# FFN forward with F tiles outermost, the activations through DRAM, and the output product in a stage of its own

## The chip, the cores and the metric

The kernel runs on one core of a Trainium2 chip. The metric is the device time of one execution in microseconds (us). TensorE (PE) multiplies, VectorE (DVE) and ScalarE (ACT) work on tiles in SBUF and PSUM, GpSimd (POOL) and SyncE (SP) issue DMA transfers here. A DMA is queued by the engine that issues it, so there are queues of SP, ACT and POOL.

## The reference

Forward and backward of one block, for L = 2048 tokens, D = 576 channels, F = 4608 hidden units and N = 128 states; inputs and outputs are bf16.

```
xn  = layernorm(u)
s   = S4 state space model: long convolution of xn with a kernel made of A, B, C, log_dt, plus Dskip * xn
ffn(x) = (silu(x @ w1) * (x @ w3)) @ w2          # w1, w3: D x F, w2: F x D
g   = silu(ffn(xn))
out = u + s * g
outputs: out and the gradients of all inputs for a given grad_out
```

## The kernel before

The phases follow each other in this order: constants, layernorm, parameters and the convolution kernel, the convolution itself by DFT blocks (phase 3; its last matmuls are L607, inv_ps), the FFN forward (phase 4, which the change rewrites), the backward pass of the state space model (phase 5), the backward pass of the FFN (phase 6: weight gradients, then input gradients). xn lies transposed in DRAM as XNT_dram. D = 576 is four blocks of 128 and a rest of 64, F is 36 tiles of 128.

Phase 4 before (L637 to L764) goes over four chunks of 512 tokens, and in each over the 36 F tiles (fi). For one F tile and each half of 256 tokens, five matmuls with w1res (L697) and five with w3c (L700) accumulate the two products in one PSUM tile gu; the last of the five uses a block whose lower 64 rows are zero. ScalarE makes the sigmoid and two bf16 copies (L704 to L706), VectorE two products (L708, L709) that give hT. Both copies go to G_dram and U_dram for phase 6. For each of the four token tiles of the chunk hT is then multiplied with this F tile's rows of w2 (w2r): 512 columns into o_main (L714) and 64 into o_tail (L718). w1 is resident (w1res), loaded at the start by 72 DMAs; w3c and w2r are loaded again in each chunk, with a memset by GpSimd for w3c's zero rows. At the end of a chunk there is an epilogue for four token tiles (L722 to L755): copies, a sigmoid (L732), eight passes on VectorE per tile that give out, gs_t and go_o (the gradients that phases 5 and 6 need, stored to GS_dram and GO_dram), and transposes of go_o (L761) that are stored to GOT_dram.

Phase 5 starts with the DFT matrices Cf, Sf and others: VectorE and ScalarE compute them by rows (L416 to L440), and PE transforms gs with them (dft_ps, L496). Phase 6 reads G_dram and U_dram (L1177, L1189), makes ph (L1209), the weight gradients pgw (L1238, L1250, and L1257 and L1259 for the last 64 rows) and the input gradient px (L1302).

`self.dma` (L77) gives its transfers to SP's and ACT's queue by turns. The order of instructions on each engine is made by a scheduler from the program's order; tiles come from pools, and a pool that is opened later can lie on the addresses of one that is closed.

Of the kernel before, what the change touches and what calls it, by code (L numbers as in the profile page):

```python
# [60 lines left out]
class K:  # L61
# [561 lines left out]
    def load_wcols(self, pool, w_ap, f0, fw, name, eng=None):  # L623
        nc, cfg = self.nc, self.cfg
        D, DT = cfg.D, cfg.DT
        t_ = pool.tile([P, DT, fw], BF16, name=name)
        nfull = D // P
        rem = D - nfull * P
        if rem > 0:
            nc.gpsimd.memset(t_[rem:P, DT - 1, :], 0.0)  # L630
        if nfull > 0:
            self.dma(t_[:, 0:nfull, :], w_ap[0:nfull * P, f0:f0 + fw].rearrange("(c p) f -> p c f", p=P), eng=eng)
        if rem > 0:
            self.dma(t_[0:rem, nfull, :], w_ap[nfull * P:D, f0:f0 + fw], eng=eng)
        return t_

    def phase4_ffn_fwd(self):  # L637
# [3 lines left out]
        TCW = min(512, L)  # L641
        NTC = L // TCW
        TS = TCW // P
        HW = TCW // 2
        assert TCW % 2 == 0 and HW <= 256
        opieces = [(0, min(512, D))] + ([(512, D - 512)] if D > 512 else [])
        assert D <= 1024
        self.G_dram = self.dram.tile([FT, P, L], BF16, name="G_dram")
        self.U_dram = self.dram.tile([FT, P, L], BF16, name="U_dram")
        self.GS_dram = self.dram.tile([P, LT, D], BF16, name="GS_dram")  # L650
        self.GO_dram = self.dram.tile([P, LT, D], BF16, name="GO_dram")
        self.GOT_dram = self.dram.tile([P, DT, L], BF16, name="GOT_dram")
# [3 lines left out]
        with self.tc.tile_pool(name="f_big", bufs=1) as big, \  # L656
                self.tc.tile_pool(name="f_w", bufs=3) as wpool, \
                self.tc.tile_pool(name="f_gu", bufs=3) as gup, \
                self.tc.tile_pool(name="f_h", bufs=2) as hpool, \
                self.tc.tile_pool(name="f_ep", bufs=2) as ep, \  # L660
                self.tc.tile_pool(name="f_ep1", bufs=2) as ep1, \
                self.tc.tile_pool(name="f_goo", bufs=TS) as goop, \
                self.tc.tile_pool(name="f_pso", bufs=TS, space=bass.MemoryType.PSUM) as pso, \
                self.tc.tile_pool(name="f_pst", bufs=1, space=bass.MemoryType.PSUM) as pst, \
                self.tc.tile_pool(name="f_psg", bufs=2, space=bass.MemoryType.PSUM) as psg, \
                self.tc.tile_pool(name="f_pstr", bufs=1, space=bass.MemoryType.PSUM) as pstr:
            xnT = big.tile([P, DT, L], BF16, name="xnT4")
            for c in range(DT):
                self.dma(xnT[:, c, :], self.XNT_dram[:, c, :])
            w1 = big.tile([P, DT, F], BF16, name="w1res")  # L670
            nfull = D // P
            rem = D - nfull * P
            if rem > 0:
                nc.vector.memset(w1[rem:P, DT - 1, :], 0.0)
            for ft in range(FT):
                if nfull > 0:
                    self.dma(w1[:, 0:nfull, ft * P:(ft + 1) * P],
                             aps["B_w1"][0:nfull * P, ft * P:(ft + 1) * P].rearrange("(c p) f -> p c f", p=P))
                if rem > 0:
                    self.dma(w1[0:rem, nfull, ft * P:(ft + 1) * P], aps["B_w1"][nfull * P:D, ft * P:(ft + 1) * P])  # L680
            for tci in range(NTC):
                t0 = tci * TCW
                o_main = [pso.tile([P, 512], FP32, name="o_main") for _ in range(TS)]
                o_tail = pst.tile([P, TS, 64], FP32, name="o_tail") if len(opieces) > 1 else None
                for fi in range(FT):
                    f0 = fi * P
                    w3c = self.load_wcols(wpool, aps["B_w3"], f0, P, "w3c")
                    w2r = wpool.tile([P, D], BF16, name="w2r")
                    self.dma(w2r[:], aps["B_w2"][f0:f0 + P, :])
                    hT = hpool.tile([P, TCW], BF16, name="hT")  # L690
                    gsp = gup.tile([P, TCW], BF16, name="g_sp")
                    usp = gup.tile([P, TCW], BF16, name="u_sp")
                    for hh in range(2):
                        tsl = slice(t0 + hh * HW, t0 + (hh + 1) * HW)
                        gu = psg.tile([P, 2, HW], FP32, name="gu")
                        for c in range(DT):
                            nc.tensor.matmul(gu[:, 0, :], lhsT=w1[:, c, f0:f0 + P], rhs=xnT[:, c, tsl],  # L697
                                             start=(c == 0), stop=(c == DT - 1))
                        for c in range(DT):
                            nc.tensor.matmul(gu[:, 1, :], lhsT=w3c[:, c, :], rhs=xnT[:, c, tsl],  # L700
                                             start=(c == 0), stop=(c == DT - 1))
                        hs = slice(hh * HW, (hh + 1) * HW)
                        sig = gup.tile([P, HW], BF16, name="sig")
                        nc.scalar.activation(out=sig[:], in_=gu[:, 0, :], func=ACT.Sigmoid)  # L704
                        nc.scalar.copy(out=gsp[:, hs], in_=gu[:, 0, :])  # L705
                        nc.scalar.copy(out=usp[:, hs], in_=gu[:, 1, :])  # L706
                        silu = gup.tile([P, HW], BF16, name="silu")
                        nc.vector.tensor_tensor(out=silu[:], in0=gsp[:, hs], in1=sig[:], op=ALU.mult)  # L708
                        nc.vector.tensor_tensor(out=hT[:, hs], in0=silu[:], in1=usp[:, hs], op=ALU.mult)  # L709
                    self.dma(self.G_dram[fi, :, t0:t0 + TCW], gsp[:])  # L710
                    self.dma(self.U_dram[fi, :, t0:t0 + TCW], usp[:])
                    for ts in range(TS):
                        (po, pw) = opieces[0]
                        nc.tensor.matmul(o_main[ts][:, 0:pw], lhsT=hT[:, ts * P:(ts + 1) * P], rhs=w2r[:, po:po + pw],  # L714
                                         start=(fi == 0), stop=(fi == FT - 1))
                        if o_tail is not None:
                            (po, pw) = opieces[1]
                            nc.tensor.matmul(o_tail[:, ts, 0:pw], lhsT=hT[:, ts * P:(ts + 1) * P], rhs=w2r[:, po:po + pw],  # L718
                                             start=(fi == 0 and ts == 0), stop=(fi == FT - 1 and ts == TS - 1))
# [697 lines left out]
```

## Time and profile before

| | before |
|---|---|
| median of three runs | 3525.78 us (3524.29 to 3532.9) |
| profiled execution | 3535.09 us, its span 3533.3 us |
| PE busy | 2430.8 us, 69% of the span |
| VectorE busy | 1961.1 us, 56% |
| ScalarE busy | 1601.8 us, 45% |
| GpSimd busy | 221.5 us, 6% |
| mean granted clock of PE | 0.774 |
| DMA | 368.13 MB, 104 GB/s in the mean |

The profile and the trace are of one execution. Busy time is the time in which an engine has an instruction; a granted clock of 1.00 is 2.4 GHz, 0.5 is 1.2 GHz. Phase 4 lies between about 802 and 1445 us of the span.

### The profile page before, as it was taken

What the parts mean: (1) busy time and instruction counts of PE and PEld (TensorE: products, weight loads), DVE (VectorE), ACT (ScalarE), POOL (GpSimd) and SP (SyncE); (2) the same over time, 40 slices, a digit from 0 to 9 for tenths busy, and PEclk for the clock granted to TensorE, in tenths of its full rate; (3) what the DMA queues carried; (4) which work ended last, traced back from release to release, by engine and by line L of the source; (5) the groups of instructions that cost most, each with busy time, mean ns of one, the idle gap of its engine ahead of it and who ended that gap; (6) DMA issues with size and microseconds to landing.
All of it is one profiled execution on the core that took longest, in us unless ns stands there. A gap on an engine that the chain in (4) does not pass through costs nothing.

```text
span 3533.3 us, 53058 instructions
## 1 busy us (share of the span) xinstructions
PE 2430.8 (69%) x20638; PEld 1645.3 (47%) x20638; DVE 1961.1 (56%) x3182; ACT 1601.8 (45%) x2617; POOL 221.5 (6%) x518
## 2 busy tenths in 40 slices
PE   2999994836988979373632111117999998973999
PEld 1444442624655656162421111105677776752777
DVE  6777777582344343847579999983444433410222
ACT  2888885402544545441106655626565665510000
POOL 1000000000000000000000000001222222210000
PEclk8555555968988999596765555558999999986999
DMA  2000000206566565301124333317544544437442
GB/s 75 20 21 21 22 22 20 108 19 180 152 177 171 157 173 155 115 1 53 42 52 114 99 100 100 98 26 212 152 139 133 145 143 132 117 95 190 166 176 78
DMA packets 431854, 368.13 MB, mean 104 GB/s; under 512 B 210929, under 2 KB 395762, under 8 KB 429426
## 3 DMA queue, kind: packets, MB, share of 16 engines
q10 hardware_dynamic: 204000, 182.79, 16.9%
q1 hardware_dynamic: 208018, 122.94, 13.5%
q0 software_dynamic: 19584, 59.00, 5.3%
q8 instruction: 162, 2.65, 0.3%
q14 instruction: 90, 0.74, 0.1%
HBM read 214.81 MB, written 133.27 MB: 99 GB/s over the span
## 4 chain that ended last, share of the span: by engine, by line
PE 50%; DVE 26%; issue 9%; DMA 7%; SPq 3%; POOL 2%; ACT 2%; ACTq 0%; POOLq 0%; DVEq 0%
PE px L1302 8%; PE o_main L714 4%; PE ph L1209 4%; PE gu L700 4%; PE gu L697 4%; PE tau_ps L353 4%; PE e_ps L356 3%; PE dft_ps L496 3%; SPq L1114 3%; DVE prodI L1006 2%; PE gk_ps L866 2%; DVE red L1014 2%; PE e_ps L365 2%; DMA out_dram<-gw 2%; PE pgw L1238 2%
## 5 line engine op out<-in xcount | busy, mean ns | idle before, releaser
L993 PE MATMUL pT<-gK,QTr 64*128 64x32 bf16 x576 | 72.6, 185 | 295.8 <-DVE QTr L979 269.5
L708 DVE TENSOR_TENSOR silu<-g_sp,sig 128x256 bf16<-128x256 bf16 x288 | 83.8, 292 | 344.1 <-ACT g_sp L705 343.7
L1302 PE MATMUL px<-w1T,ggc 128*128 128x288 bf16 x1152 | 238.1, 289 | 49.5 <-DMA w3T<-in_B_w_dram 41.8
L697 PE MATMUL gu<-xnT,w1res 128*128 128x256 bf16 x1440 | 229.8, 275 | 46.3 <-ACT u_sp L706 33.6
L1302 PE MATMUL px<-w3T,guc 128*128 128x288 bf16 x1152 | 237.8, 289 | 32.3 <-DMA guc<-GU_dram 20.2
L1250 PEld LDWEIGHTS <-xn_bf 128*128 128x128 bf16 x2304 | 226.0, 99 | 58.1 <-issue 30.3
L704 ACT ACTIVATE sig<-gu 128x256 bf16<-128x256 f32 x288 | 110.5, 384 | 272.9 <-PE gu L700 234.7
L700 PE MATMUL gu<-xnT,w3c 128*128 128x256 bf16 x1440 | 228.8, 275 | 0.0
L993 PEld LDWEIGHTS <-QTr 64*128 64x128 bf16 x1152 | 65.0, 101 | 319.1 <-DVE QTr L979 273.7
L1209 PE MATMUL ph<-go_oT,w2T 128*128 128x512 bf16 x720 | 169.5, 381 | 60.8 <-DMA w2T<-w2r 58.2
L714 PE MATMUL o_main<-w2r,hT 128*128 128x512 bf16 x576 | 188.3, 395 | 9.6 <-DVE hT L709 2.4
L1253 DVE CAST gw<-pgw 128x256 bf16<-128x256 f32 x144 | 60.1, 423 | 229.5 <-DMA out_dram<-gw 125.9
L1306 DVE TENSOR_TENSOR gx<-px,gx 128x288 f32<-128x288 f32 x32 | 13.1, 452 | 306.6 <-PE px L1302 200.6
L1319 ACT ACTIVATE t<-gx 128x576 f32<-128x576 f32 x16 | 10.9, 683 | 374.5 <-DVE gx L1306 374.5
L1238 PE MATMUL pgw<-go_o,h_n 128*128 128x288 bf16 x1152 | 165.1, 286 | 0.0
L697 PEld LDWEIGHTS <-w1res 128*128 128x128 bf16 x1440 | 131.6, 98 | 71.1 <-issue 35.6
L1250 PE MATMUL pgw<-gg_n,xn_bf 128*128 128x256 bf16 x1152 | 133.4, 276 | 27.1 <-DVE gw L1253 27.1
L1302 PEld LDWEIGHTS <-ggc 128*128 128x128 bf16 x1152 | 113.6, 99 | 80.1 <-issue 50.6
L700 PEld LDWEIGHTS <-w3c 128*128 128x128 bf16 x1440 | 132.9, 99 | 30.6
L353 PE MATMUL tau_ps<-SELQ,thp 64*128 64x512 f32 x144 | 143.2, 1096 | 0.3 <-ACT WiT L242 0.3
L1302 PEld LDWEIGHTS <-guc 128*128 128x128 bf16 x1152 | 113.5, 99 | 63.4 <-DMA guc<-GU_dram 20.8
L356 PE MATMUL e_ps<-SELQ,rho 64*128 64x512 f32 x144 | 137.5, 1057 | 0.0
(358 smaller groups left out, 6667.8 us busy)
## 6 DMA issues: line engine op xcount, KB each, us to landing
rep_t<-RT_dram SPq DMA_DIRECT2D x72, 256.0 KB, 4.1
rep_r<-RT_dram ACTq DMA_DIRECT2D x72, 256.0 KB, 3.9
gate<-G_dram POOLq DMA_DIRECT2D x36, 512.0 KB, 4.7
up<-U_dram POOLq DMA_DIRECT2D x36, 512.0 KB, 6.2
GU_dram<-guT ACTq DMA_DIRECT2D x36, 512.0 KB, 3.3
GG_dram<-ggT ACTq DMA_DIRECT2D x36, 512.0 KB, 6.5
ggc<-GG_dram ACTq DMA_DIRECT2D x8, 2304.0 KB, 8.8
guc<-GU_dram ACTq DMA_DIRECT2D x8, 2304.0 KB, 14.2
```

The source lines that it names most:

```text
L353: nc.tensor.matmul(pt[:], lhsT=self.thp[rows, c, :], rhs=SELQ[rows, cols], start=True, stop=True)
L356: nc.tensor.matmul(pe[:], lhsT=self.rho[rows, c, :], rhs=SELQ[rows, cols], start=True, stop=True)
L496: nc.tensor.matmul(pt[:, 0:pw], lhsT=mat[:, tt, kc * P:(kc + 1) * P], rhs=src_fn(tt)[:, po:po + pw], start=(tt == 0), stop=(tt == KT - 1))
L697: nc.tensor.matmul(gu[:, 0, :], lhsT=w1[:, c, f0:f0 + P], rhs=xnT[:, c, tsl], start=(c == 0), stop=(c == DT - 1))
L700: nc.tensor.matmul(gu[:, 1, :], lhsT=w3c[:, c, :], rhs=xnT[:, c, tsl], start=(c == 0), stop=(c == DT - 1))
L704: nc.scalar.activation(out=sig[:], in_=gu[:, 0, :], func=ACT.Sigmoid)
L714: nc.tensor.matmul(o_main[ts][:, 0:pw], lhsT=hT[:, ts * P:(ts + 1) * P], rhs=w2r[:, po:po + pw], start=(fi == 0), stop=(fi == FT - 1))
L993: nc.tensor.matmul(pT[:, gi, kind, :], lhsT=lhs[rows, dl, :], rhs=rhs[rows, dp, :], start=True, stop=True)
L1209: nc.tensor.matmul(ph[:, q * 512:(q + 1) * 512], lhsT=w2T[:, c, :], rhs=go_oT[:, c, hh * HL + q * 512:hh * HL + (q + 1) * 512], start=(c = ...
L1238: nc.tensor.matmul(pgw[pi_][:, 0:pw], lhsT=h_ns[fl][:, tt, :], rhs=go_o[:, tt, po:po + pw], start=(tt == 0), stop=(tt == LT - 1))
L1250: nc.tensor.matmul(pw_[:, 0:GW], lhsT=self.xn_bf[:, tt, c * P:(c + 1) * P], rhs=nat[:, tt, :], start=(tt == 0), stop=(tt == LT - 1))
L1302: nc.tensor.matmul(px[pi_][:, 0:pw], lhsT=act[:, fi, k * P:(k + 1) * P], rhs=wT[:, fi, po:po + pw], start=(fi == 0 and ai == 0), stop=(fi ...
```

## The change

Phase 4 is split in two. The first part (phase4_hidden) takes one F tile after the other, and for each all 2048 tokens in two halves of 1024: the two products are made in PSUM tiles pg and pu (two banks each, two buffers each), with matmuls of 512 columns (L683). The rest of 64 rows of D is no longer padded with zeros: w1's 64 rows lie on partitions 0 to 63 and w3's on 64 to 127 of one tile (wtail), xnT's last 64 rows are loaded to both halves of the partitions, and the K=64 matmuls for pg (L686) and pu (L688) use the two row halves of the array. ScalarE makes Silu directly (L690) and copies pu (L692), VectorE copies pg (L691) and makes the product (L693) for 2048 tokens. The product is stored to H_dram (L694, SP's queue, runs of 512 bytes), g_t and u_t to G_dram and U_dram (POOL's queue, 512 KB each). The weights of four F tiles come in one group of loads on SP; w2 is loaded into w2res (41 KB per partition) by nine loads on POOL's queue.

The second part (phase4_output) loads H_dram again, 256 tokens of all F tiles at a time (hc, eight loads of 2304 KB, three buffers), and for each of 16 token tiles does 72 matmuls of 288 columns with w2res (L727). The epilogue follows for each tile, with five transposes a tile (L752). The buffers of phase 5's DFT matrices lie on addresses of w2res; before, they lay on addresses of w1res and xnT4.

```diff
-            for tci in range(NTC):
...
                 for fi in range(FT):
-                    w3c = self.load_wcols(wpool, aps["B_w3"], f0, P, "w3c")
-                    self.dma(w2r[:], aps["B_w2"][f0:f0 + P, :])
...
-                    for hh in range(2):
-                        for c in range(DT):
-                            nc.tensor.matmul(gu[:, 0, :], lhsT=w1[:, c, f0:f0 + P], rhs=xnT[:, c, tsl],
-                                             start=(c == 0), stop=(c == DT - 1))
...
-                    for ts in range(TS):
-                        nc.tensor.matmul(o_main[ts][:, 0:pw], lhsT=hT[:, ts * P:(ts + 1) * P], rhs=w2r[:, po:po + pw],
-                                         start=(fi == 0), stop=(fi == FT - 1))
...
+            for fi in range(FT):
+                if fl == 0:
+                    for w in ("B_w1", "B_w3"):
+                        nc.sync.dma_start(out=wm[w][:], in_=aps[w][0:nfull * P, f0:f0 + GRP * P].rearrange(
...
+                    nc.gpsimd.dma_start(out=self.w2res[:, fi:fi + GRP, :],
...
+                for hh in range(L // HL):
+                    for (w, pt) in (("B_w1", pg), ("B_w3", pu)):
+                        for c in range(nfull):
+                            for (o, t0) in qs:
+                                nc.tensor.matmul(pt[:, o:o + 512], lhsT=wm[w][:, c, cs], rhs=xnT[:, c, t0:t0 + 512],
+                    for (o, t0) in qs:
+                        nc.tensor.matmul(pg[:, o:o + 512], lhsT=wt[0:rem, cs], rhs=xnT[0:rem, nfull, t0:t0 + 512],
+                        nc.tensor.matmul(pu[:, o:o + 512], lhsT=wt[rem:P, cs], rhs=xnT[rem:P, nfull, t0:t0 + 512],
+                    nc.scalar.activation(out=s_t[:, hs], in_=pg[:], func=ACT.Silu)
+                    nc.vector.tensor_copy(out=g_t[:, hs], in_=pg[:])
+                    nc.scalar.copy(out=u_t[:, hs], in_=pu[:])
+                nc.vector.tensor_tensor(out=h_t[:], in0=s_t[:], in1=u_t[:], op=ALU.mult)
+                nc.sync.dma_start(out=self.H_dram[:, :, fi, :].rearrange("c p l -> p c l"),
+                nc.gpsimd.dma_start(out=self.G_dram[fi], in_=g_t[:])
+                nc.gpsimd.dma_start(out=self.U_dram[fi], in_=u_t[:])
...
+            for i in range(LT):
+                if k == 0:
+                    nc.sync.dma_start(out=hc[:], in_=self.H_dram[i // (TC // P)])
...
+                for fi in range(FT):
+                    for pi_, (po, pw) in enumerate(pieces):
+                        nc.tensor.matmul(po_[:, pi_, 0:pw], lhsT=hc[:, fi, k * P:(k + 1) * P],
+                                         rhs=self.w2res[:, fi, po:po + pw], start=(fi == 0), stop=(fi == FT - 1))
```

On PE, inside a chunk, the kernel before has these rows (numbers of tiles behind a name are those of the program):

```order
L700 LDWEIGHTS w3c
L700 MATMUL gu<-xnT_6805,w3c 128x256
L697 LDWEIGHTS w1res
L697 MATMUL gu<-xnT_6805,w1res 128x256
L697 LDWEIGHTS w1res
L697 MATMUL gu<-xnT_6805,w1res 128x256
L714 LDWEIGHTS hT
L714 MATMUL o_main<-w2r,hT 128x512
L718 LDWEIGHTS hT
L718 MATMUL o_tail<-w2r,hT 128x64
L714 LDWEIGHTS hT
L714 MATMUL o_main<-w2r,hT 128x512
L718 LDWEIGHTS hT
L718 MATMUL o_tail<-w2r,hT 128x64
L697 LDWEIGHTS w1res
L697 MATMUL gu<-xnT_6805,w1res 128x256
```

The products of the next half stand between those of hT with w2r, and half of the matmuls with hT have 64 columns. In the changed kernel PE has these rows at the end of one half and the start of the next:

```order
L683 LDWEIGHTS wmB_w_6798
L683 MATMUL pu<-xnT_6789,wmB_w_6798 128x512
L686 LDWEIGHTS wtail
L686 MATMUL pg<-xnT_6789,wtail 128x512
L688 LDWEIGHTS wtail
L688 MATMUL pu<-xnT_6789,wtail 128x512
L686 LDWEIGHTS wtail
L686 MATMUL pg<-xnT_6789,wtail 128x512
L688 LDWEIGHTS wtail
L688 MATMUL pu<-xnT_6789,wtail 128x512
L683 LDWEIGHTS wmB_w_6796
L683 MATMUL pg<-xnT_6789,wmB_w_6796 128x512
```

All matmuls have 512 columns; the K=64 ones stand in turns, pg and pu, between those of two halves, and no product with w2 is left here.

On VectorE, at the end of phase 4, the kernel before has the last tile of a four-tile epilogue (24 rows of the other three tiles stand ahead of it) and then rows of the DFT matrices:

```order
L742 TENSOR_TENSOR t1e<-s_t_15374,g 128x576
L747 TENSOR_TENSOR gs_t<-go_t,g 128x576
L744 TENSOR_TENSOR o_15380<-t1e,x_t 128x576
L750 SCALAR_TENSOR_TENSOR e<-o_sb,g 128x576
L753 TENSOR_TENSOR t1e<-go_t,s_t_15374 128x576
L752 TENSOR_TENSOR e<-e,sgo 128x576
L425 TENSOR_SCALAR g_u<-g_u 128x512
L755 TENSOR_TENSOR go_o<-t1e,e 128x576
L427 SCALAR_TENSOR_TENSOR g_fr<-g_tau,g_u 128x512
L416 TENSOR_SCALAR g_prod<-irow,tcolv 128x512
```

The DFT rows L425, L427 and L416 stand behind the four tiles. In the changed kernel the same place reads:

```order
L467 TENSOR_SCALAR tcolv<-pcol 128x1
L458 TENSOR_SCALAR w_10761<-w_10761 128x1
L810 TENSOR_TENSOR gsxn<-gs,xn_bf 128x576
L735 TENSOR_TENSOR g<-po,sgo 128x576
L416 TENSOR_SCALAR g_prod<-irow,tcolv 128x512
L736 SCALAR_TENSOR_TENSOR e<-po,g 128x576
L744 TENSOR_TENSOR gs_t<-go_t,g 128x576
L739 TENSOR_TENSOR e<-e,sgo 128x576
L746 TENSOR_TENSOR g<-s_t_10628,g 128x576
L741 TENSOR_TENSOR go_o<-gos,e 128x576
L748 TENSOR_TENSOR o_10721<-g,x_t 128x576
L419 TENSOR_SCALAR g_q<-g_prod 128x512
```

Only one tile's epilogue stands here; a product with gs (gsxn) and the first DFT rows stand ahead of it and in it.

On GpSimd the changed kernel has these rows where the kernel before has only memsets of w3c, 144 of them:

```order
L668 DMA w2res<-in_B_w_dram 128x4x576 x8
L697 DMA U_dram<-u_t 128x2048
L696 DMA G_dram<-g_t 128x2048
L668 DMA w2res<-in_B_w_dram 128x4x576
L721 DMA x_t<-in_A_u_dram 128x576
L722 DMA go_t<-in_grad_out_dram 128x576
L723 DMA s_t_8979<-S_dram 128x576
L721 DMA x_t<-in_A_u_dram 128x576
L722 DMA go_t<-in_grad_out_dram 128x576
```

Eight of nine loads of w2res stand ahead of the first store of an F tile, and loads of the epilogue's inputs for the first tiles stand behind it.

## Rows read from the trace of the kernel before

**Rows 1.** Windows, start of the stage; us, then busy us (count) per engine, clock, DMA.

```profile
804.50:845.00 40.50, 11.37 (x59) 7.14 (x59) 3.35 (x9) 4.88 (x13) 0.40 (x2) 0.58 0.81 211
845.00:960.00 115.00, 111.94 (x889) 73.01 (x890) 36.85 (x127) 58.66 (x192) 6.37 (x32) 1.00 0.61 164
960.00:1000.00 40.00, 23.77 (x172) 15.55 (x172) 27.67 (x56) 17.34 (x49) 0.99 (x5) 0.74 0.66 190
```

**Rows 2.** Timeline of PE, start of the stage; start us, us, instruction, [idle before].

```profile
802.22 0.29 PE L607 MATMUL inv_ps<-Yi,SiPN 128*128 128x288 bf16 x1
813.06 1.23 PE L697 MATMUL gu<-xnT,w1res 128*128 128x256 bf16 x5 [10.56 <-DMA w1res<-in_B_w_dram]
...
837.16 0.37 PE L697 MATMUL gu<-xnT,w1res 128*128 128x256 bf16 x1 [20.34 <-ACT u_sp L706]
```

**Rows 3.** Timeline of ScalarE and its DMA queue, same place.

```profile
807.80 27.06 ACTq L81 DMA_DIRECT2D w1res<-in_B_w_dram  x36
834.89 1.28 ACT L704 ACT_TABLE_LOAD   x1 [156.99 <-DMA w1res<-in_B_w_dram]
```

**Rows 4.** Timeline of PE, end of the stage.

```profile
1421.45 0.19 PE L718 MATMUL o_tail<-w2r,hT 128*128 128x64 bf16 x1
1429.64 0.29 PE L761 MATMUL ptr<-ident_bf,go_o 128*128 128x128 bf16 x1 [8.00 <-DVE go_o L755]
...
1493.41 1.12 PE L496 MATMUL dft_ps<-gs,Cf 128*128 128x288 bf16 x4 [7.28 <-ACT Ghr L499]
```

**Rows 5.** Timeline of VectorE, end of the stage.

```profile
1422.82 1.42 DVE L740 TENSOR_TENSOR g<-o_sb,sgo 128x576 f32<-128x576 f32 x2
...
1443.55 0.42 DVE L425 TENSOR_SCALAR g_u<-g_u 128x512 f32<-128x512 f32 x1
...
1489.06 0.42 DVE L425 TENSOR_SCALAR g_u<-g_u 128x511 f32<-128x511 f32 x1
```

**Rows 6.** Chain that ended last, two pieces; start us, us, engine, tile, line, count.

```profile
2511.72 6.91 PE ph L1209 x32
...
3259.86 266.34 PE px L1302 x2159
```

**Rows 7.** Timeline of PE, weight gradients of phase 6.

```profile
2588.37 0.71 PE L1250 MATMUL pgw<-gg_n,xn_bf 128*128 128x256 bf16 x5
2589.01 0.30 PE L1257 MATMUL pgw<-gg_n,xn_bf 128*64 128x256 bf16 x1
2589.01 0.30 PE L1259 MATMUL pgw<-gu_n,xn_bf 128*64 128x256 bf16 x1
...
2590.67 0.27 PE L1259 MATMUL pgw<-gu_n,xn_bf 128*64 128x256 bf16 x1
2590.88 0.51 PE L1122 MATMUL ptr<-ident_bf,hT 128*128 128x128 bf16 x6
```

**Rows 8.** Groups of instructions, shapes apart; count, busy us, mean ns, idle before.

```profile
L1191 DVE TENSOR_TENSOR hT<-silu,up 128x2048 bf16<-128x2048 bf16 x36 | 43.8, 1217 | 33.1 <-DMA up<-U_dram 18.4 <-ACT silu L1180 14.6
...
L1126 ACT COPY gu_n<-ptr 128x1024 bf16<-128x1024 bf16 x36 | 37.1, 1030 | 5.4 <-PE ptr L1122 2.8 <-DVE ggT L1217 2.6
...
L1253 DVE CAST gw<-pgw 128x256 bf16<-128x256 f32 x144 | 60.1, 423 | 229.5 <-DMA out_dram<-gw 125.9 <-PE pgw L1250 87.3 <-PE pgw L1259 9.7
...
L740 DVE TENSOR_TENSOR g<-o_sb,sgo 128x576 f32<-128x576 f32 x16 | 11.7, 751 | 5.2 <-ACT sgo L732 5.2
```

**Rows 9.** DMA issues; count, KB each, median us from issue to landing.

```profile
up<-U_dram POOLq DMA_DIRECT2D x36, 512.0 KB, 6.2
GU_dram<-guT ACTq DMA_DIRECT2D x36, 512.0 KB, 3.3
GG_dram<-ggT ACTq DMA_DIRECT2D x36, 512.0 KB, 6.5
ggc<-GG_dram ACTq DMA_DIRECT2D x8, 2304.0 KB, 8.8
...
xnT<-XNT_dram ACTq DMA_DIRECT2D x3, 512.0 KB, 6.9
```

More of the change, by code (lines that the diff above doesn't have):

```diff
@@ L619, in phase3_body, with phase4_hidden @@
                 Yprev = (Yr, Yi)
[L623 to L635, printed above, removed]
-    def phase4_ffn_fwd(self):
+    def phase4_ffn_fwd(self):
+        cfg = self.cfg
+        D, DT, L, LT, FT = cfg.D, cfg.DT, cfg.L, cfg.LT, cfg.FT
+        self.TC4 = 256
+        self.G_dram = self.dram.tile([FT, P, L], BF16, name="G_dram")
+        self.U_dram = self.dram.tile([FT, P, L], BF16, name="U_dram")
+        self.H_dram = self.dram.tile([L // self.TC4, P, FT, self.TC4], BF16, name="H_dram")
+        self.GS_dram = self.dram.tile([P, LT, D], BF16, name="GS_dram")
+        self.GO_dram = self.dram.tile([P, LT, D], BF16, name="GO_dram")
+        self.GOT_dram = self.dram.tile([P, DT, L], BF16, name="GOT_dram")
+        with self.tc.tile_pool(name="o_w", bufs=1) as wpool:
+            self.w2res = wpool.tile([P, FT, D], BF16, name="w2res")
+            self.phase4_hidden()
+            self.phase4_output()
+    def phase4_hidden(self):
         nc, cfg = self.nc, self.cfg
@@ L640, in phase4_ffn_fwd @@
         aps = self.aps
[L641 to L651, printed above, removed]
@@ L653, in phase4_ffn_fwd, with phase4_output @@
+    def phase4_output(self):
+        nc, cfg = self.nc, self.cfg
+        D, DT, L, LT, F, FT = cfg.D, cfg.DT, cfg.L, cfg.LT, cfg.F, cfg.FT
+        aps = self.aps
+        TC = self.TC4
+        pieces = self.dpieces()
         out0 = aps["out_0"].flatten_outer_dims()
```

176 lines of the change are left out of this document (77 added, 99 removed).

## The prediction

> **What bounds the kernel now.** I read the windows of the FFN stage first, then the timelines of PE at its two ends, then VectorE and ScalarE at the same places. In the middle of a token chunk PE is busy 111.94 of 115 us at the full 2.4 GHz (granted clock 1.00) while the DMA engines are busy 0.61 of the time at 164 GB/s [rows 1]. So inside a chunk the stage is bound by TensorE: 889 matmuls in 115 us, and at 28 per F tile and chunk (20 of 256 columns, 4 of 512, 4 of 64) that is 3.62 us for 7424 columns. The columns alone are 3.09 us at 2.4 GHz. Where two chunks meet, PE is busy 23.77 of 40 us at clock 0.74, and VectorE 27.67 [rows 1]; that happens three times. At the start PE finishes the convolution at 802.5, begins at 813.06, does 20 matmuls and stands still until 837.16 [rows 2]: it waits for an eviction by ScalarE, whose queue is issuing loads of w1res for 27 us, so that the sigmoid's table is loaded only at 834.89 [rows 3]. At the end the last o_tail is at 1421.45, and the transform of phase 5 (dft_ps) starts in earnest at 1493.41 [rows 4]: first VectorE does the epilogue of four tiles from 1422.82, then, from 1443.55 to after 1489, the DFT matrices [rows 5].
>
> From the end of the convolution (802.5) to dft_ps (1493.4) it is 690.9 us. Everything behind hangs on dft_ps, so what this stretch loses the end of the program loses. I price the stretch of the changed kernel.
>
> **Start: 11.5 us.** The 72 loads of w1 on two queues go, and with them the stall to 837. What remains is the wait for xnT. Each of its 512 KB pieces took 6.9 us to land [rows 9], beside other loads. Now the first weights are there early, but 4.7 MB of w2 start on GpSimd's queue at the same moment as 2.6 MB of xnT. I let the first 4.09 us half (below) end at about 818, so an effective start at 814, near the old 813.06. Lower bound 810 (6.9 us after issue); upper bound: all 7.3 MB at the 211 GB/s of the busiest window [rows 1] are 35 us, effective start 834, or +20 us.
>
> **Hidden stage: 294 us.** For each of 36 F tiles and two halves of 1024 tokens PE does 16 matmuls of 512 columns, and then four of K=64 in pairs, rows 0 to 63 beside rows 64 to 127. A 512-column matmul costs 6.91/32 = 0.216 us [rows 6], so 16 are 3.456 us. For pairs the nearest row is of phase 6, where two column halves (L1257, L1259) start in the same 10 ns and 16 pairs of 256 columns run from 2589.01 to 2590.78, that is 0.11 us a pair, the price of one [rows 7]. Row pairs are not in the trace; I take them as concurrent like these: 2 x 0.216 = 0.432. If they ran one after the other it would be 0.864 (a rival). Entering and leaving the pairs costs something: the last L1250 starts at 2588.37 + 4 x 0.11 = 2588.81 and the first pair at 2589.01, 0.20 instead of 0.11; the last pair starts at 2590.67 and the next full matmul at 2590.88, 0.21 instead of 0.11 [rows 7]. That is 0.1 us a switch, 0.2 a half, 14.4 us in the stage. Bounds 0 and 0.3.
>
> The Trainium skill ("TensorEngine Tiling (Array Packing)", Key Properties) speaks against the change here: a change of tiling mode drains TensorE, and this kernel would change it 144 times, where zero-padded tails change it never. The trace agrees that there is a gap, and gives its length, which the page doesn't: by these rows the rule costs 14 us of the sum, while free switches would give 3351.
>
> One half is 3.456 + 0.432 + 0.2 = 4.09 us, the stage 72 x 4.09 = 294.4; 280 without the switches.
>
> The cover of the rest: ScalarE does Silu and a copy of 128x1024 each half, about 1.03 us each by the copy of that size [rows 8], 2.1 of 4.09. VectorE casts 128x1024 from PSUM: 0.423 for 256 columns [rows 8], so at most 1.69, and half of a 1.22 us product [rows 8], 2.3 of 4.09. Both PSUM tiles have two buffers, so neither is late. The DMA queues carry per F tile (8.18 us) three stores of 512 KB and 295 KB of weights, 1.87 MB, or 228 GB/s. The busy windows give 164 GB/s at a share of 0.61 and 211 at 0.81 [rows 1], which scales to 260 to 269 at full share, with smaller pieces than these. So DMA is hidden with a margin of an eighth; this is the thinnest cover of the sum.
>
> **Bubble: 18 us.** The output stage needs all 36 F tiles of the first 256 tokens. Behind the last matmul come Silu and copy 2.06, product 1.22, the H store 3.3 (GU_dram row, same size) and the load of hc 8.8 (ggc row, same shape) [rows 8, 9], with 0.6 for semaphores 16 us. PE stands idle, and after such a wait its clock was 1.2 GHz (granted clock 0.58 in that window [rows 1]): five matmuls took 1.23 us at 813.06 and 0.71 at 2588.37 [rows 2, 7]. I add 2 us for that. Bounds 14 to 24; a store like GG_dram is 3.2 more.
>
> **Output: 154 us.** 1152 matmuls of 128x288 with two buffers of PSUM. The same shape with streamed operands ran 2159 times in 266.34 us, 0.1234 each [rows 6]: 142.2. The 80 transposes are 80 x 0.056 = 4.5. They sit some 4.8 us into the next tile and need go_o, which VectorE has after a sigmoid and six passes of 0.75 [rows 8], about 5.25: 15 waits of 0.45, so 7 us (0 to 15). A pair of tiles lasts 18 us and its hc is loaded in 8.8, so this load is hidden.
>
> **Tail: 52 us.** Behind the last output matmul stands one tile's epilogue instead of four: a sigmoid of 0.7 (estimate from the copy of 1024 columns) and seven passes of 0.75, 6 us. Then the DFT matrices, 49.9 us from 1443.55 to 1493.41 [rows 4, 5]; some products with gs, which stood between them, now stand ahead, so 46.4 (40 to 50). They still cannot start earlier: their buffers lie over those of w2res, which is read to the last matmul.
>
> **Sum.** 11.5 + 294.4 + 18 + 153.7 + 52.4 = 530.0 against 690.9: 160.9 us less. The profiled execution took 3535.1, so 3374; it lies 9.3 above the median of the runs (3525.8), and against that I predict 3365. About a quarter of the gain is columns: 1,069,056 before and 995,328 after are 31 us at 2.4 GHz; the rest is the start, the three chunk ends, the epilogue and the gap of 0.53 us in each of the 144 F-tile steps. The alternation of SP and ScalarE queues is shifted by one in phases 5 and 6, so that loads change queue; I take 0, with 8 us either way.
>
> **Rivals.**
> *Tails run one after the other.* Speaks for it: no row shows row pairs. Against: the column pairs. Price 72 x 0.432 = 31 us: 3396.
> *DMA paces the hidden stage.* For it: 228 GB/s are asked for, and no FFN window showed more than 211. Against: the share there was 0.81. At 211 GB/s an F tile takes 8.85 us, +24: 3389; at 200, 9.35 us, +42: 3407.
> *Slower or no change: G and U stores on GpSimd's queue go strictly one after the other.* Buffers are two, so the evictions of F tile fi+2 wait for the stores of fi, and PE for the evictions. At 3.3 each they hide; at the 6.2 of up<-U_dram, the row of that queue and size, 12.4 us a tile, +152: 3517; at the 6.5 of GG_dram 13.0, +173.5: 3538. The gain is gone when an F tile takes (294.4 + 160.9)/36 = 12.65 us, so from 6.33 us a store. Against it: the loads on this queue are two at a time already.
>
> **How the numbers follow.** 0.3% (10.6 us) is about what a measurement of this kernel can tell from no change. My forecast 0.75, with a range of its own of 3345 to 3390; serial tails 0.10; DMA at about 200 to 211 GB/s 0.10; stores in series 0.05, of which 0.02 near no change and 0.03 slower. Faster 0.95, same 0.02, slower 0.03. The range goes from free switches, no wait for go_o and an early start (3365 - 14 - 7 - 4 = 3340, with some of the queues' 8 us 3335) to serial tails with the late start (3396 + 20 = 3416, rounded to 3420).
>
> **What would show it.** Start: first L683 at about 810 to 814, no stall of 20 us. Hidden: L683 at a pitch of 0.216, L686 and L688 starting together, a step of 8.2 us an F tile, clock 1.00, DMA over 210 GB/s. Bubble: PE idle some 16 us once, released by hc. Output: last L727 at about 1280. Tail: dft_ps at about 1332, 161 earlier. It would be wrong if L686 and L688 don't overlap, if the first matmul of a half waits for ScalarE or VectorE (whose own release is then a store landing), if xnT lands past 825, or if a stage behind dft_ps changes its length.

## The result

The changed kernel takes 3371.77 us (median, 3371.12 to 3374.96), the kernel before 3528.19 beside it; the ratio is 0.9558, with a 95% interval of 0.9541 to 0.9574. The forecast was 3365 with a range of 3335 to 3420. The profiled execution took 3372.14, its span 3370.4 us against 3533.3. The page gives, against the values of the table ahead:

```profile
PE 2351.0 (70%) x19198; PEld 1532.3 (45%) x19198; DVE 1926.4 (57%) x2713; ACT 1468.8 (44%) x1878; POOL 263.5 (8%) x503
```

PE is 80 us less busy, at the same mean clock (0.775). The timeline of PE at the start of the stage (start, duration, instruction, idle time before) answers to [rows 2]:

```profile
801.99 0.29 PE L607 MATMUL inv_ps<-Yi,SiPN 128*128 128x288 bf16 x1
807.82 1.86 PE L683 MATMUL pg<-xnT,wmB_w 128*128 128x512 bf16 x4 [5.54 <-DMA xnT<-XNT_dram]
...
819.00 0.42 PE L686 MATMUL pg<-xnT,wtail 64*128 64x512 bf16 x1
819.01 0.42 PE L688 MATMUL pu<-xnT,wtail 64*128 64x512 bf16 x1
...
823.67 1.90 PE L683 MATMUL pg<-xnT,wmB_w 128*128 128x512 bf16 x8
```

No stall of 20 us is left, but three waits for pieces of xnT (9.7 us in all); the first tails run at 819.0, L686 and L688 within 0.01 us of each other. From 823.67 one half of 1024 tokens follows the other; at the end of the stage and the start of the next the same timeline reads:

```profile
1106.34 1.90 PE L683 MATMUL pg<-xnT,wmB_w 128*128 128x512 bf16 x8
...
1127.91 17.53 PE L727 MATMUL po<-w2res,hc 128*128 128x288 bf16 x121 [17.40 <-DMA hc<-H_dram]
```

Between 823.67 and 1106.34 there are 69 halves, 4.097 us each, so the 72 halves of the hidden stage are 295.0 us long. Counted back from 823.67 its effective start is 815.5, and it ends at 1110.4. Then PE waits 17.4 us for hc. The windows in the stage (PE, PEld, VectorE, ScalarE, GpSimd, clock, DMA share, GB/s) answer to [rows 1]:

```profile
820.00:900.00 80.00, 80.00 (x391) 31.31 (x390) 34.88 (x30) 38.21 (x40) 15.42 (x29) 1.00 0.75 258
```

PE is busy throughout, clock 1.00, DMA at 258 GB/s in this window and 219 from 1000 to 1100 us. The end of the output stage and the tail, again from PE's timeline, answer to [rows 4]:

```profile
1271.45 8.99 PE L727 MATMUL po<-w2res,hc 128*128 128x288 bf16 x72
1280.71 0.57 PE L752 MATMUL ptr<-ident_bf,go_o 128*128 128x128 bf16 x5 [0.27 <-DVE go_o L741]
1281.22 4.22 PE L727 MATMUL po<-w2res,hc 128*128 128x288 bf16 x33
1285.36 0.65 PE L812 MATMUL gds_ps<-gsxn,ones_col 128*1 128x288 bf16 x4
...
1341.86 1.12 PE L496 MATMUL dft_ps<-gs,Cf 128*128 128x288 bf16 x4 [7.01 <-ACT Ghr L499]
```

A token tile takes 9.77 us: 72 matmuls in 8.99, five transposes in 0.51, and 0.27 of waiting for go_o. The last L727 ends at 1285.4, dft_ps starts in earnest at 1341.86. Two of the waits of PE between 802 and 1345 us (us in total, times, longest):

```profile
PE pg L683 <- DMA xnT<-XNT_dram: 9.7, 3, 5.5
...
PE ptr L752 <- DVE go_o L741: 7.7, 15, 4.0
```

| stretch, us | forecast | measured |
|---|---|---|
| start, to the effective start | 11.5 | 13.2 |
| hidden stage | 294.4 | 295.0 |
| bubble | 16 | 17.5 |
| output, with the slow first matmuls | 155.7 | 157.4 |
| tail to dft_ps | 52.4 | 56.5 |
| sum, end of L607 to dft_ps | 530.0 | 539.6 |
| all behind dft_ps | 2039.9 (as before) | 2028.5 |

The stretch is 151.3 us shorter than before (690.9), of 156.4 by the medians. The last row compares two single executions, and that of the kernel before lies 6.9 us above its median. No run separates what the chunk ends and the F-tile steps of the kernel before contribute to the gain.

### The profile page after: what moved, and what is told of

It reads as the page before. It is cut to its first block, busy times and chain, and to the rows that moved or that the text cites. A ratio compares the mean times of both kernels' runs of the same rounds, so it can differ in the third digit from the quotient of the medians.

```text
span 3370.4 us, 46694 instructions
## 1 busy us (share of the span) xinstructions
PE 2351.0 (70%) x19198; PEld 1532.3 (45%) x19198; DVE 1926.4 (57%) x2713; ACT 1468.8 (44%) x1878; POOL 263.5 (8%) x503
## 3 DMA queue, kind: packets, MB, share of 16 engines
q10 hardware_dynamic: 117888, 129.08, 12.3%
## 4 chain that ended last, share of the span: by engine, by line
PE 40%; DVE 26%; issue 18%; DMA 7%; POOL 3%; SPq 3%; ACT 2%; ACTq 0%; POOLq 0%; DVEq 0%
PE px L1293 8%; PE ph L1200 4%; PE tau_ps L353 4%; PE e_ps L356 4%; PE dft_ps L496 3%; SPq L1105 3%; DVE red L1005 2%; PE gk_ps L857 2%; DVE prodI L997 2%; PE e_ps L365 2%; DMA out_dram<-gw 2%; PE pgw L1241 2%; PE tau_ps L362 2%; PE inv_ps L607 2%; PE pgw L1229 2%
## 5 line engine op out<-in xcount | busy, mean ns | idle before, releaser
L691 DVE CAST g_t<-pg 128x1024 bf16<-128x1024 f32 x72 | 88.2, 1224 | 182.3 <-ACT s_t L690 182.3
L683 PEld LDWEIGHTS <-wmB_w 128*128 128x128 bf16 x1152 | 107.4, 98 | 161.6 <-issue 44.2
L727 PE MATMUL po<-w2res,hc 128*128 128x288 bf16 x1152 | 146.4, 289 | 17.4 <-DMA hc<-H_dram 17.4
L1241 PE MATMUL pgw<-gg_n,xn_bf 128*128 128x256 bf16 x1152 | 135.0, 279 | 26.7 <-DVE gw L1244 26.7
L690 ACT ACTIVATE s_t<-pg 128x1024 bf16<-128x1024 f32 x72 | 73.8, 1024 | 168.7 <-PE pu L688 168.7
L683 PE MATMUL pg<-xnT,wmB_w 128*128 128x512 bf16 x576 | 138.5, 383 | 9.7 <-DMA xnT<-XNT_dram 9.7
L683 PE MATMUL pu<-xnT,wmB_w 128*128 128x512 bf16 x576 | 138.0, 383 | 0.0
L1241 PE MATMUL pgw<-gu_n,xn_bf 128*128 128x256 bf16 x1152 | 137.5, 273 | 0.0
```

What stands on the lines that cost most here:

```text
L683: nc.tensor.matmul(pt[:, o:o + 512], lhsT=wm[w][:, c, cs], rhs=xnT[:, c, t0:t0 + 512], start=(c == 0), stop=False)
L691: nc.vector.tensor_copy(out=g_t[:, hs], in_=pg[:])
L727: nc.tensor.matmul(po_[:, pi_, 0:pw], lhsT=hc[:, fi, k * P:(k + 1) * P], rhs=self.w2res[:, fi, po:po + pw], start=(fi == 0), stop=(fi == F ...
L1241: nc.tensor.matmul(pw_[:, 0:GW], lhsT=self.xn_bf[:, tt, c * P:(c + 1) * P], rhs=nat[:, tt, :], start=(tt == 0), stop=(tt == LT - 1))
```

## The experiments

Each time is a median; ratios are to the kernel before on the same chip, with their 95% interval. The changed kernel's ratio is 0.9558.

**The tails: are the row pairs concurrent, and what does a switch cost?** Three kernels, each with one edit to the matmuls of the 64 remaining rows.

```diff
-lhsT=wt[0:rem, cs],  rhs=xnT[0:rem, nfull, t0:t0 + 512]   # pg
-lhsT=wt[rem:P, cs],  rhs=xnT[rem:P, nfull, t0:t0 + 512]   # pu
+lhsT=wt[:, cs],      rhs=xnT[:, nfull, t0:t0 + 512]       # tails_padded; rows 64 to 127 of xnT are zero
+lhsT=wt3[:, cs],     rhs=xnT[:, nfull, t0:t0 + 512]
...
+lhsT=wt[0:rem, cs],  rhs=xnT[0:rem, nfull, t0:t0 + 512]   # tails_serial; both on rows 0 to 63
+lhsT=wt3[0:rem, cs], rhs=xnT[0:rem, nfull, t0:t0 + 512]
```

> The changed kernel with its K=64 tails as full 128-row matmuls (the lower 64 rows of xnT's last block are zero), one after the other, so no change of tiling mode. By the rows a half then takes 16 x 0.216 + 4 x 0.216 = 4.32 us instead of 4.096: 72 x 0.224 = +16 us, 3388. If the two switches of a half cost what the pairs save, 3372; if row pairs were not concurrent at all, it would be faster than 3372, by up to 14 us.

> The changed kernel with both K=64 tails on rows 0 to 63, so that they cannot run beside each other but the mode still changes twice a half. If the gain of the tails is their running side by side, a half takes 3.456 + 0.864 + 0.2 = 4.52 us, +0.43 x 72 = +31 us: 3403. Rival: K=64 matmuls are cheaper by themselves and the pairing does nothing: 3372.

tails_padded takes 3388.28 us (0.9603, 0.9589 to 0.9616), tails_serial 3405.84 (0.9654, 0.9641 to 0.9667): 16.5 and 34.1 above the changed kernel, where 16 and 31 were worked out. The timeline of PE in tails_padded:

```profile
883.39 1.89 PE L687 MATMUL pg<-xnT,wmB_w 128*128 128x512 bf16 x8
...
887.28 0.38 PE L690 MATMUL pg<-xnT,wtail 128*128 128x512 bf16 x1
...
887.71 1.89 PE L687 MATMUL pg<-xnT,wmB_w 128*128 128x512 bf16 x8
```

A half is 887.71 - 883.39 = 4.32 us, four more matmuls at 0.216 and no gap. In tails_serial:

```profile
880.86 1.90 PE L684 MATMUL pg<-xnT,wmB_w 128*128 128x512 bf16 x8
...
884.42 0.39 PE L687 MATMUL pg<-xnT,wtail 64*128 64x512 bf16 x1
884.65 0.38 PE L689 MATMUL pu<-xnT,wtail 64*128 64x512 bf16 x1
...
885.39 1.90 PE L684 MATMUL pg<-xnT,wmB_w 128*128 128x512 bf16 x8
```

The two tails of a pair start 0.22 to 0.23 us apart, the price of a full matmul each, and the half is 4.53 us. So a K=64 matmul is not cheaper by itself; what pays is that two run at once on the two row halves. The Trainium skill ("TensorEngine Tiling (Array Packing)", Key Properties) says that different tiles work independently, and the trace agrees for row halves, at 0.01 us between the two starts.

In the third kernel every second half does its tails first, so that tails of two halves stand together:

```diff
+                    if hh == 0:
+                        full()
+                        tails()
+                    else:
+                        tails()
+                        full()
```

> The changed kernel with the tails of every second half ahead of its full matmuls instead of behind them, so that two halves' tails stand together and the tiling mode changes twice an F tile instead of four times. If a switch costs 0.1 us wherever it stands, a step of 8.19 us becomes 7.99 and the hidden stage loses 7.2 us: 3364.5. Rival: what I read as the switch is the exposed load of the tails' weights, which stays: 3372.

It takes 3364.54 us (0.9531, 0.9514 to 0.9548), as expected to 0.1 us. Its timeline of PE:

```profile
883.27 1.89 PE L684 MATMUL pu<-xnT,wmB_w 128*128 128x512 bf16 x8
885.09 0.39 PE L689 MATMUL pg<-xnT,wtail 64*128 64x512 bf16 x1
...
885.75 0.38 PE L689 MATMUL pg<-xnT,wtail 64*128 64x512 bf16 x1
...
886.06 1.90 PE L684 MATMUL pg<-xnT,wmB_w 128*128 128x512 bf16 x8
```

Of the eight matmuls from 883.27 the last starts at 884.78, and 0.31 us pass to the first pair instead of 0.216; the pairs follow each other without a gap, also between the two halves, and 0.31 pass again from the last pair to 886.06. A switch is 0.095 us, and it is the changing of the mode that costs: with half as many changes half of it is gone. That is the drain which the Trainium skill names in the same section; the runs give its length.

**The start.** 

```diff
-                    nc.gpsimd.dma_start(out=self.w2res[:, fi:fi + GRP, :],
+                    nc.sync.dma_start(out=self.w2res[:, fi:fi + GRP, :],
```

> The changed kernel with the loads of w2res on SP's queue behind the weights of their own group, instead of eight at once on GpSimd's queue at the start. Theory: they delay xnT, whose last pieces land at about 816 to 819 us. Without them xnT lands at about 812, the first tails start at about 815 instead of 819.0, and the time falls by about 4 us to 3368. Rival: xnT's own 2.6 MB and its queues set that time; then 3372 and the first tails stay at 819.

3375.02 us (0.956, 0.9543 to 0.9576): no gain. But the edit did not do what was meant: SP issued six of the nine loads between 807.15 and 822 us, right behind xnT. The window of the start:

```profile
807.00:820.00 13.00, 6.89 (x21) 2.38 (x23) 0.00 (x0) 1.03 (x2) 3.46 (x7) 0.74 1.03 341
```

The DMA engines are full there (341 GB/s; in the changed kernel 330 between 804 and 820). Whether xnT alone would land earlier is not told by this run.

For the start of the kernel before, its small w1 loads were taken off ScalarE's queue:

```diff
                     self.dma(w1[:, 0:nfull, ...], ...
-                             ...)                    # by turns, these came to SP's queue
+                             ..., eng=nc.sync)       # and stay there
-                    self.dma(w1[0:rem, nfull, ...], aps["B_w1"][nfull * P:D, ...])
+                    self.dma(w1[0:rem, nfull, ...], aps["B_w1"][nfull * P:D, ...], eng=nc.gpsimd)
```

> The kernel before with its 36 small loads of w1's last rows on GpSimd's queue, so that ScalarE issues none of the w1res loads; nothing else changed. Theory: ScalarE's first evictions then follow the first matmuls at about 815 us, the stall of 20.34 us before 837.16 goes, and with it 20 us: 3508. Rival: the DMA engines pace the start (w1, w3 and xnT at 211 GB/s), so other waits take its place and 10 us or less are won: 3520.

3518.88 us against 3529.25 beside it, 0.9969 (0.9957 to 0.9981): 10 us, the rival's number. The waits of PE in its FFN stage, and the start of dft_ps:

```profile
PE gu L697 <- ACT u_sp L706: 14.1, 9, 3.1
PE gu L697 <- DMA w1res<-in_B_w_dram: 12.4, 1, 12.4
PE gu L700 <- DMA w3c<-in_B_w_dram: 12.4, 1, 12.4
```

```profile
1489.19 1.12 PE L496 MATMUL dft_ps<-gs,Cf 128*128 128x288 bf16 x4 [7.28 <-ACT Ghr L499]
```

ScalarE is free in time and the waits for u_sp fall from 33.6 to 14.1 us in all. But a wait of 12.4 us for w3c is new, and that for w1res is 12.4 instead of 10.6, so 5.3 us of waiting are gone. The stretch from the end of L607 (804.0) to dft_ps is 685.2 us, 5.7 shorter than before. So by the traces a quarter, by the medians half of the 20 us went; the rest of the stall that I put down to ScalarE's queue was covered by loads that came no earlier.

**Is DMA near its limit in the hidden stage?**

```diff
+                nc.gpsimd.dma_start(out=self.G2_dram[fi], in_=g_t[:])
```

> The changed kernel with a third store of 512 KB per F tile on GpSimd's queue (g_t once more, to a DRAM tile that nobody reads; the outputs are unchanged): 2.39 MB in a step of 8.19 us, 292 GB/s instead of 228. The prediction put the limit of the queues at 260 to 269 GB/s, worked out from the windows of before; then a step takes 8.9 to 9.2 us and the time rises by 25 to 36 us, to 3397 to 3408. Rival: the limit is nearer to the 300 GB/s that the queues moved while xnT and w2res were loaded (812 to 820 us); then 3372 to 3380, and DMA was never near to being the bound.

3372.29 us (0.9549, 0.9527 to 0.9571): the third store costs nothing. Its window of the stage:

```profile
820.00:1110.00 290.00, 290.00 (x1414) 112.48 (x1413) 125.67 (x106) 136.26 (x142) 60.90 (x115) 1.00 0.84 294
```

294 GB/s at a share of 0.84, PE busy for all of the 290 us, clock 1.00. The DMA engines' limit is not at the 260 to 269 GB/s of the prediction, and the cover is thicker than an eighth.

**The bubble.** In hc_early the first hc tile has buffers that are free during the hidden stage; 32 of its 36 F tiles are loaded then, four behind it.

```diff
+                if fi == NA + 1:   # NA = 32
+                    nc.scalar.dma_start(out=self.hc0[:, 0:NA, :], in_=self.H_dram[0, :, 0:NA, :])
...
+            nc.sync.dma_start(out=self.hc0[:, NA:FT, :], in_=self.H_dram[0, :, NA:FT, :])
```

> The changed kernel with the first hc tile in buffers of its own, F tiles 0 to 31 of it loaded during the hidden stage and only the last four behind it. The bubble of 17.4 us between the stages is evictions, product, store and load in series. Theory: the load of 8.5 us leaves the chain and 64 matmuls (8 us) run beside the rest, so some 3 us of waiting for the last four F tiles remain and some 14 us of idle time go: 3358. Rival: the wait is for the stores to land (H_dram behind G_dram and U_dram), the load waits for all of them and only its length falls: about 3365.

3388.2 us (0.96, 0.9582 to 0.9618), 16 us slower. The waits of PE in it:

```profile
PE pg L686 <- DMA wmB_w<-in_B_w_dram: 22.4, 1, 22.4
PE ptr L760 <- DVE go_o L749: 20.9, 16, 13.2
```

The bubble went as expected (2.4 and 1.0 us of waiting are left), but the pool of hc pushed the weights' buffers onto those of the convolution's last products, so the first weights were issued at 805.30 instead of 783.66 and came late (22.4 us), and the first epilogue waited 13.2 us for its inputs. With the pools in another order (weights of two F tiles a group, clear of those buffers; input tiles with buffers of their own):

> hc_early took the bubble away (2.4 and 1.0 us of waiting in place of 17.4) but moved the first weights onto buffers that the convolution still reads (22.4 and 5.2 us of waiting at the start) and left the inputs of the first epilogue late (13.2 us). Here the weights come two F tiles a group and lie clear of those buffers, and the input tiles have buffers of their own, so that only the bubble differs from the changed kernel. Theory: -14 us, 3358. Rival: the first weights' loads and the rest of hc_early's losses come from the layout as such, and 3372 or more stays.

3359.45 us (0.9512, 0.9499 to 0.9525), 12.3 faster than the changed kernel. Its output stage starts like this on PE's timeline:

```profile
1114.96 16.47 PE L736 MATMUL po<-w2res,hc 128*128 128x288 bf16 x121 [2.73 <-ACT u_t L696]
```

2.73 us of waiting for the last u_t and then 121 matmuls without a break, where the changed kernel waits 17.40. Its effective start is 13.2 us behind the last L607, as in the changed kernel, so nothing but the bubble and the slow first matmuls behind it differs up to there.

**The tail.** dft_kept makes the DFT matrices once, for the convolution, and keeps them through phase 4 (hc has two buffers; gK2 lies in the place of the convolution kernel KT).

```diff
-            with self.tc.tile_pool(name="b_mats", bufs=1) as matp:
-                self.build_dft_mats(matp)
-                self.phase5_scopeA(gK2)
+        self.phase5_scopeA(gK2)
+        self.mat_ctx.close()
```

> The changed kernel without the second making of the DFT matrices: those of the convolution stay in SBUF through phase 4 (hc gets two buffers instead of three, and gK2 lies in KT's place), so phase 5 computes none. Theory: behind the last output matmul the 49 us of matrices on VectorE are the whole tail but one tile's epilogue; dft_ps starts some 10 us behind the last output matmul instead of 56.5, so 3372 - 47 = 3325, or lower if blocks of gs that are ready are transformed earlier. Rival: the tail is set by gs (store and load again) and its products with xn; then the gain is 20 us or less, 3352.

3345.4 us (0.9468, 0.9444 to 0.9492): 26 us less, not 47. Its PE timeline at the end of the output stage, and SP's queue there:

```profile
1281.56 4.22 PE L726 MATMUL po<-w2res,hc 128*128 128x288 bf16 x33
...
1303.88 0.64 PE L496 MATMUL dft_ps<-gs,Cf 128*128 128x288 bf16 x2 [12.20 <-DMA gs<-GS_dram]
...
1356.88 0.64 PE L854 MATMUL gk_ps<-Zr,CiL 128*64 128x288 bf16 x2 [5.20 <-DVE Zr L527]
```

```profile
1300.70 6.03 SPq L81 DMA_DIRECT2D gs<-GS_dram  x8
```

The tail falls from 56.5 to 18.2 us (1285.7 to 1303.88). Now gs is late: its loads are issued at 1300.70 only, 9 us behind the last epilogue, and PE waits 12.20 us for them; their buffers lie over those of the output stage. The next matmuls behind the transforms (gk_ps) start like this in the changed kernel:

```profile
1383.55 0.69 PE L857 MATMUL gk_ps<-Zr,CiL 128*64 128x288 bf16 x2 [5.19 <-DVE Zr L527]
```

So of the 38 us at the start of dft_ps 26.7 are left at gk_ps: the transforms take 53.0 us to there instead of 41.7, and up to 1318 they stand between matmuls of gds_ps, which the changed kernel has behind it by then. At the start PE waits 8.3 us for weights, which again need the convolution's buffers, in place of the 9.7 for xnT; this loses nothing. So the DFT matrices were the tail, as the theory has it, and behind them the rival's wait stood ready.

**All of it together.** combined has alternate tails, kept matrices, hc's first tile and gs in KT's place, and two F tiles of weights a group, so that xnT and the weights can land before the convolution ends.

> The changed kernel with what the runs so far point to: tails alternate; DFT matrices kept; weights of two F tiles a group, so that xnT and the weights lie clear of the convolution's last buffers and xnT can land before the convolution ends; the first hc in KT's place, 32 of its F tiles loaded during the hidden stage; gs in KT's place too, so that its loads don't wait for the output stage's buffers. By the pieces: alternate tails -7, early xnT -13 (first tails at once instead of 16.7 us behind the last L607), bubble -14, tail -45 (dft_ps right behind the last output matmul, some 10 us for the last gs): 3372 - 79 = 3293. If the pieces hide one another (gs late, inputs of the first tile late as with hc_early): 3320.

3329.89 us (0.9429, 0.9407 to 0.9452), 42 us faster than the changed kernel and the fastest of all, but 37 short of the sum of its pieces. dft_ps starts at 1282.2, less than 3 us behind the last output matmul. About half of what was lost is at the start. VectorE, at the end of the convolution, and ScalarE's and SP's queues there:

```profile
804.29 0.46 DVE L610 TENSOR_TENSOR s_t<-inv_ps,xdt 128x288 bf16<-128x288 f32 x1 [6.94 <-DMA S_dram<-s_t]
...
817.29 0.82 DVE L610 TENSOR_TENSOR s_t<-inv_ps,xdt 128x288 bf16<-128x288 f32 x2 [11.19 <-DMA S_dram<-s_t]
```

```profile
785.30 1.35 ACTq L81 DMA_DIRECT2D xnT<-XNT_dram  x3
797.17 0.32 ACTq L81 DMA_DIRECT2D S_dram<-s_t  x1
```

```profile
804.34 6.08 SPq L668 DMA_DIRECT2D wtail<-in_B_w_dram  x1
...
812.88 0.35 SPq L81 DMA_DIRECT2D S_dram<-s_t  x1
```

xnT is issued at 785.30, early as meant. But then a store of the convolution's result, issued at 797.17, lands 7.0 us later, and VectorE waits 6.94 us for it to free s_t. The next one stands on SP's queue behind weights: issuing one load of wtail takes 6.08 us, the store goes out at 812.88 only, and VectorE waits 11.19 us. PE waits for VectorE, and the first hidden half starts at 818.16, behind the effective start of the changed kernel (815.5) and some 16 us behind what was expected. The early loads delayed the work that they were to be hidden behind.

The other half lies behind the start of dft_ps. PE and VectorE there:

```profile
1282.18 1.14 PE L496 MATMUL dft_ps<-KT,Cf 128*128 128x288 bf16 x4 [2.38 <-DVE e L752]
...
1296.88 1.12 PE L826 MATMUL gds_ps<-gsxn,ones_col 128*1 128x288 bf16 x4 [6.91 <-DVE gsxn L824]
...
1342.05 0.64 PE L871 MATMUL gk_ps<-Zr,CiL 128*64 128x288 bf16 x2 [5.20 <-DVE Zr L527]
```

```profile
1296.37 0.46 DVE L824 TENSOR_TENSOR gsxn<-KT,xn_bf 128x576 bf16<-128x576 bf16 x1 [10.90 <-DMA GOT_dram<-gT]
```

dft_ps starts 59.7 us earlier than in the changed kernel, gk_ps only 41.5. The products with gs wait 10.90 us for the output stage's last store of gT, which they don't read (so probably for a buffer; no run tests that), PE waits 6.91 us for them, and then the transforms stand between matmuls of gds_ps, as in dft_kept.

**The queues of phases 5 and 6.** One line at the start of phase 5 moves the alternation by one:

```diff
+        self._dma_i += 1
```

> The kernel before with the alternation of SP's and ScalarE's queues moved on by one at the start of phase 5, and nothing else. In the changed kernel everything behind dft_ps is 11.4 us shorter than before, nearly all of it (12 us) at the first input gradients (px). Theory: this comes only from which queue the transfers of phases 5 and 6 use, not from phase 4. Then this kernel takes about 3528 - 11 = 3517 us, with the long wait of px for w3T (10.0 us before 3259.86) gone. Rival: it is a consequence of phase 4's own work; then 3528.

> The changed kernel with the same move of the alternation, so that phases 5 and 6 use the queues as the kernel before did. Theory of the queues: 3372 + 11 = 3383 us, the wait of px for w3T back. Rival (the shorter phase 6 belongs to phase 4's work): 3372.

before_flip takes 3526.01 us against 3530.19 (0.999, 0.9979 to 1.0001), which is no difference that can be told, after_flip 3382.01 (0.9579, 0.9563 to 0.9595; single runs from 3372.97 to 3389.64). The waits of px for w3T in the changed kernel, and in after_flip:

```profile
PE px L1293 <- DMA w3T<-in_B_w_dram: 8.4, 3, 7.4
```

```profile
PE px L1294 <- DMA w3T<-in_B_w_dram: 16.1, 3, 11.2
```

The profiled execution of after_flip is the slowest of its five. In it the wait for w3T is 7.7 us longer. Another 9.1 us lie in phase 4's output stage (from 1128.69 to 1295.23), which the edit doesn't touch. The wait of ScalarE that is new there:

```profile
ACT sgo L732 <- DMA GS_dram<-gs_t: 25.7, 5, 6.1
```

Phase 5's loads of gs stand between the sigmoids on ScalarE. With the turns moved by one, ScalarE has a load whose store is still on its way, waits for it with up to 6.1 us, and the sigmoid, go_o and PE come late. So the old order costs the changed kernel some 10 us in the median, but half of that is not what the theory says.

The new order does not give the old kernel 11 us. And before_w1_off_act, which has the order of the kernel before and its phases 5 and 6, takes 2027.3 us behind dft_ps (3516.5 - 1489.19), 12.6 less than the 2039.9 of before; before_flip takes 2035.2. So single executions of the same phases with the same queues differ by as much as the 11.4 us that were to be explained. By the medians some 5 us of them are left, and their cause stays open.

## Why the prediction was right

**Hidden stage.** 294.4 forecast, 295.0 measured. All three parts hold: 0.216 a matmul, pairs at the price of one, 0.095 for a switch where I took 0.1. tails_padded, tails_serial and tails_alternate change one part each and come out within some 3 us of the sum.

**Cover.** Neither ScalarE, VectorE nor a store stopped PE once in this stage. A store on GpSimd's queue lands in this time (count, KB each, median us), one of u_t in 3.1:

```profile
G_dram<-g_t POOLq DMA_DIRECT2D x36, 512.0 KB, 4.1
```

G_dram's 4.1 is below the 6.33 at which stores in series would have taken the gain away, and even one after the other the two would take 7.2 us of a step of 8.19, so the rival on the other side was far off. The DMA limit was read too low: scaling GB/s by the busy share, from windows with many small pieces, gave 260 to 269, and 294 ran at 0.84.

**Bubble.** Right within 1.5 us. The chain that ended last has these pieces in it (start, duration):

```profile
1115.55 3.51 DMA G_dram<-g_t
...
1119.18 8.49 DMA hc<-H_dram
```

The load takes 8.49 us where 8.8 was forecast. It is issued 5.2 us behind the last product (1114.0) instead of 3.3: the store of G, issued last, lands at 1119.06. SP's queue waited 3.2 us for the store of H and then

```profile
SPq L717 <- DMA G_dram<-g_t: 1.2, 1, 1.2
```

The load of hc doesn't read G_dram. hc's pool is opened when that of g_t is closed, so this last 1.2 us is probably a wait for g_t's buffer; no run tests it by itself. The 0.6 us for semaphores in the sum has no row; 0.24 us pass from the landing of hc to the first matmul. hc_early2 shows that the series is the cause: without it 12.3 of the 17.4 us go.

**Output.** 1.7 us over, from errors that cancel: the five transposes of a tile cost 0.51 us and not 0.28 (15 times, +3.1), the waits for go_o were 14 of 0.27 and not 15 of 0.45 (-3.3), the 72 matmuls of a tile take 0.11 more to the end of the last than 72 x 0.1234 (+1.6), and the slow first ones cost 2.4 and not 2.

**Tail.** 56.5 for 52.4, the largest term that was mis-sized. VectorE behind the last matmul:

```profile
1290.87 0.75 DVE L748 TENSOR_TENSOR o<-g,x_t 128x576 bf16<-128x576 f32 x1
...
1291.88 0.45 DVE L810 TENSOR_TENSOR gsxn<-gs,xn_bf 128x576 bf16<-128x576 bf16 x1
```

The sigmoid and the epilogue of one tile end at 1291.6, 6.2 us behind the last L727, where 6 was forecast; from there it is 50.3 us to dft_ps, where 46.4 was. Only one of the 14 products with gs (gsxn) that stood between the matrices before stands ahead now; 13 still stand between them, from 1291.88 to 1310.1, some 0.44 us each. The step that failed is "some products with gs ... now stand ahead", which I had read from the first rows of the order and not counted.

**Start.** 13.2 for 11.5: the last pieces of xnT landed later, and the first tails ran at 819.0, so that the first half ended at 819.6 and not 818.

**Behind dft_ps.** The stretch was 9.6 us longer than forecast, and all behind it 11.4 shorter, nearly all of this where px starts; I had taken 0, with 8 either way. The two cancel, and that the 3372.1 of the profiled execution stands so near to 3374 is luck. It is no step that was right or wrong: the sum took 2039.9 from one execution of the kernel before, 6.9 us above its median, and by the medians some 5 of the 11.4 us are left.

**What bounds the kernel before.** The stall of 20 us at its start was read as ScalarE's queue alone. By before_w1_off_act that is half of it at most.

## What to carry to other kernels

Price a rewritten stage by the pitch of its instructions from the old trace, then add what stands in series between stages: here the pitch was right to 0.2%, and the 10 us of error lay in the ends. A remainder of 64 rows is worth pairing on the two row halves if it can be paired with another remainder of the same kind, and the changes of mode are worth grouping. Before a stall is put down to one cause, ask what would come next in its place; three times here (w1 off ScalarE, matrices kept, xnT early) a second wait stood right behind the first and took about half of the gain, or with xnT all of it. And before a difference between two single traces is explained, look at how much other traces of the same code differ there: here 12.6 us, more than the 11.4 that two runs were spent on.

## What the runs showed of the hardware

The DMA engines moved 294 GB/s through a whole stage at a busy share of 0.84 without delaying anything, and 330 to 341 GB/s in bursts. With many loads of weights on their way (combined), issuing one load of 32 KB took SP's queue 6.08 us, where the first of the same form had taken 0.48 at 790.61; a store behind it came that much later, and it was seen as a wait of the engine that needed the store's buffer. A change of TensorE's tiling mode cost 0.095 us each way, about the same into and out of row halves as the 0.09 and 0.10 that [rows 7] have for column halves.
